# A fused attention and two-layer feed-forward kernel: 29 of 36 second-layer weight pieces converted inside the second layer, three a step, and used straight from SBUF

## The chip, the cores and the metric

One NeuronCore of one Trainium2 chip runs the whole program; the other cores are idle. The metric is the time of one execution on the device in microseconds (us), and the number compared is the median of several runs. Engines are called as in the profile: PE is TensorE (matmuls; PEld is its weight load), DVE is VectorE, ACT is ScalarE, POOL is GpSimd, SP is SyncE, which issues the DMAs. SBUF is the on-chip memory, PSUM the accumulators that PE writes, DRAM the memory off the core.

## The reference

Four batches of 512 tokens and 32 state rows pass through an attention block, then through two feed-forward layers. The first has 2048 hidden features and a softplus, the second 1536 hidden features, gated.

```python
def _moe_ref(x, w_in, w_out):                       # d_model 512, d_ff 2048
    h = x @ w_in
    g = np.maximum(h, 0.0) + np.log1p(np.exp(-np.abs(h)))
    return (g @ w_out).astype(np.float32)

def _moe2_ref(x, w_gate, w_val, w_out):             # d_model 512, d_ff 1536
    g = x @ w_gate
    silu = g * (1.0 / (1.0 + np.exp(-g)))
    val = x @ w_val
    return (silu * val @ w_out).astype(np.float32)

def reference(**kwargs):
    ...
    x = np.ascontiguousarray(attn_out.transpose(0, 2, 1, 3)).reshape(B * S, H * D)
    x = _moe_ref(x=x, **moe_kwargs)
    return _moe2_ref(x=x, **moe2_kwargs)
```

The weight matrices arrive as float64 and have to be turned into numbers that the engines can multiply; that conversion is what the change moves.

## The kernel before, in words

**Arithmetic.** PE multiplies in a reduced format (float32r). To keep float32 accuracy every operand is held as two parts, a high part and a low part (the remainder), and each product is three matmuls (`mm3`, L90): high by high, low weight by high, high weight by low. Making a pair costs one ACT copy for the high part and one subtraction for the low part (`low`, L93), on POOL for all weights.

**Weight pieces.** A raw piece is a 128x512 block of float64 words (512 KB) in SBUF, loaded by SP. Its conversion has named steps: `size` (ACT, L133 or L135), `head` and `tail` (DVE integer operations on the two 32-bit words), `high` (ACT, L164), `low` (POOL). There are two ways to convert. The first, used in the first layer, takes one head and two tails on DVE (L144, L155, L158). The second, called `slope`, takes one head and one tail (L139, L151). A gate piece (`gv`) of the second layer also needs `sums` (four 128x128 combinations of its quarters, L205; on DVE in the slope way, else on POOL) and `split_sums` (ACT, then POOL): the second layer multiplies two by two blocks with seven products in place of eight, and these are the combined weights. An output piece (`w2`) has no sums. For each of the 12 feature blocks f of the second layer there are two gate pieces, gv f_0 and gv f_1, and one output piece, w2 f: 36 in all.

**First layer.** 64 units (4 chunks of hidden features, 4 batches, 4 feature blocks each), each with a product into `ph` and one into `py`. Between chunks and batches DVE adds `yacc<-py` (L511) and makes `m` (L93), an operand of PE's next `ph`. The list EARLY puts 18 second-layer pieces at chosen units.

**Second layer.** Two passes of 12 steps (two batches a pass). Each step runs seven products of 6 matmuls on PE, in the order P1, P5, P2, P6, two output products (`po`), P7, state, two output products, P4, P3; steps 0 and 1 have a shorter order. P1, P6, P7 and P4 go into `px`, P5 and P3 into `pz`, P2 into `py`. ACT copies `px` after P1 (cA, L1025), after P6 (cB, L1054) and after P7 (cC, L1061); the next product into `px` has to wait for the copy. DVE adds `py` to cA (L1051), which ACT puts through SiLU (L1056), adds `pz` to cC (L1065) and, in the next step, finishes cA (L1069) and cB (L1077); POOL multiplies (L985). A step takes about 17 us. P5 of step n multiplies the operands T_0s and T_1s by split_gv n_0 and split_gv n_1.

The other 18 pieces are converted in steps 0 to 8, two a step. All 36 are stored to DRAM (`gv_d`, `w2_d`), and every step of both passes loads its operands back from there (`load_gw`, `load_w2`), into 8 `gw` and 4 `w2` slots. In steps 10, 12, 13, 14 and 16 a job named OutSums makes combined output weights for the second pass: two adds on DVE (`w2t`, L265), four on POOL (`w2u`, L276), then two high parts on ACT and two low parts on POOL (`w2o`). In steps 9 to 11 the operands of the second pass are combined as well (L527 and L531 on DVE, L529 and L533 on POOL).

**Order.** On DVE, ACT, POOL and SP the instructions run in the order in which the code is written (`manual_schedule`), through hooks: `at(n, kind, fn)` for units, `at2(n, kind, fn)` for steps, with conv0 to conv3 as the four points of a step. An instruction that waits holds all behind it on its engine.

Of the kernel before, what the change touches and what calls it, by code (L numbers as in the profile page):

```python
# [9 lines left out]
F32R = mybir.dt.float32r  # L10
# [6 lines left out]
P = 128  # L17
# [20 lines left out]
def attention_moe_moe2_kernel(  # L38
# [21 lines left out]
    NCK = F1 // CH  # L60
# [31 lines left out]
    def low(eng, o, whole, high):  # L92
        eng.tensor_tensor(out=o, in0=whole, in1=high.bitcast(F32), op=ALU.subtract)  # L93
# [22 lines left out]
    class Piece:  # L116
# [44 lines left out]

        def high(self):
            self.out = slot([P, 2, 512], F32R, self.tag, self.name)
            nc.scalar.activation(self.out[:, 0, :], self.t, AF.Copy)  # L164
# [17 lines left out]
    class GatePiece(Piece):  # L182
        def __init__(self, f, i, slope):
            cols = slice(f * P, (f + 1) * P)
            views = [w[(h + i) * P:(h + i + 1) * P, cols] for h in (0, 2) for w in (w_gate, w_val)]
            super().__init__(views, "made", f"gv{f}_{i}", "raw", slope)
            self.f, self.i = f, i
            if i == 0:
                gv_d[f] = dram.tile([P, 2, 2, 2, 512], F32, tag=f"gv{f}", name=f"gv{f}_d")

        def low(self):
            super().low()
            nc.sync.dma_start(out=gv_d[self.f][:, self.i, 0], in_=self.out.bitcast(F32))
# [13 lines left out]
        def split_sums(self):  # L207
            o = slot([P, 2, 512], F32R, "made", f"split_{self.name}")
            nc.scalar.activation(o[:, 0, :], self.s, AF.Copy)  # L209
            low(nc.gpsimd, o[:, 1, :], self.s, o[:, 0, :])  # L210
            nc.sync.dma_start(out=gv_d[self.f][:, self.i, 1], in_=o.bitcast(F32))

    class OutPiece(Piece):
        def __init__(self, f, slope):
            super().__init__([w_out2[f * P:(f + 1) * P, :]], "made", f"w2{f}", "raw", slope)
            self.f = f
            w2_d[f] = dram.tile([P, 2, 512], F32, tag=f"w2{f}", name=f"w2{f}_d")

# [12 lines left out]
    def second_piece(j, slope=False):  # L231
        f, part = divmod(j, 3)
        return OutPiece(f, slope) if part == 2 else GatePiece(f, part, slope)
# [504 lines left out]
    with tc.manual_schedule(engines={ENG.PE}):  # L738
# [63 lines left out]
        def at(n, kind, fn, *args):  # L802
            hooks.setdefault((n, kind), []).append((fn, args))
# [45 lines left out]
        EARLY = [(c * UC + n, 0) for c in range(NCK - 1) for n in ((2, 3, 6, 7, 10, 14) if c else (11, 14, 15))]  # L849
        EARLY += [((NCK - 1) * UC + n, 0 if n % 4 else 2) for n in (0, 1, 2)]  # L850
        for j, (n, late) in enumerate(EARLY):
            at_weights(n, late, made, (j,), second_piece)
            at(n + late + 1, "pool", lambda j=j: made[j,].sums())
            at(n + late + 2, "act", lambda j=j: made[j,].split_sums())
# [19 lines left out]
        for n in range(2):  # L874
            at(NU - 3 + n, "load", load_w2, n)
# [45 lines left out]
        for k, j in enumerate(range(len(EARLY), 3 * NF)):  # L921
            n, half = divmod(k, 2)

            def begin(j=j):
                made[j,] = second_piece(j, True)

            def step(name, j=j):
                return lambda: getattr(made[j,], name)()

            at2(n - 1, f"load{half}", begin)  # L930
            for late, names in enumerate((("head", "size"), ("tail",), ("high", "low"), ("sums",), ("split_sums",))):
                t = 4 * n + 2 * half + late + (late == 4)
                for name in names:
                    own = t // 4 >= 2 and t % 4 == 0 and name in ("size", "high", "low", "split_sums")
                    at2(t // 4, "copied" if own else f"conv{t % 4}", step(name))
# [196 lines left out]
```

## Time and profile before

| | value |
|---|---|
| median of 3 runs (lowest, highest) | 732.83 us (731.96, 732.92) |
| the profiled execution | 732.92 us, span 731.1 us |
| PE busy | 710.4 us, 97% of the span |
| DVE, ACT, POOL busy | 484.2, 331.0, 412.6 us (66%, 45%, 56%) |
| granted clock of PE, mean over the span | 0.993 |
| moved by DMA | 159.54 MB, mean 218 GB/s |
| loads of gate operands from DRAM, `gw<-gv_d` | 96 of 512 KB, 6.9 us from issue to landing |

The profiled execution is 0.09 us above the median, and 1.8 us of it lie outside the span. Busy time counts an instruction from its start to its end; the time in which an engine waits for another is idle.

### The profile page before, as it was taken

Reading aid. Unit: us, or ns where it says so; the run is one execution under the profiler, and the core shown is the slowest. Engines: PE = TensorE matmul, PEld = TensorE weight load, DVE = VectorE, ACT = ScalarE, POOL = GpSimd, SP = SyncE. Lnnn points to the kernel's source line nnn. Section 1 sums busy time; section 2 is a strip of 40 time slices with the busy share of each in tenths; the row PEclk is TensorE's granted clock in tenths of the full one; section 3 lists DMA queues with packets and bytes.
Section 4 is the critical chain, followed back from the end, with each engine's and each line's share of the span. In section 5 each row is a group of like instructions: output and inputs, shape, how many; then the busy total and the mean of one; then the engine's idle time right before and its main releaser. Section 6 shows DMA issues by size and latency. Waiting matters only on the chain.

```text
span 731.1 us, 10299 instructions
## 1 busy us (share of the span) xinstructions
PE 710.4 (97%) x3690; PEld 569.6 (78%) x3690; DVE 484.2 (66%) x689; ACT 331.0 (45%) x612; POOL 412.6 (56%) x349
## 2 busy tenths in 40 slices
PE   4899999999999999999999999999999999999997
PEld 1467877788777777788888888888888888888886
DVE  4884577888667866458476757665575665675564
ACT  3776365544445544434554344442443434333231
POOL 2477538877547765744265445455766567254352
PEclk9899999999999999999999999999999999999999
DMA  9930134655545535480389997879669997849503
GB/s 342 408 129 10 48 115 138 201 205 179 162 131 189 188 120 161 161 301 0 122 280 330 373 362 278 327 260 337 207 251 386 345 338 279 296 144 328 168 12 116
DMA packets 55395, 159.54 MB, mean 218 GB/s; under 512 B 6192, under 2 KB 18480, under 8 KB 55344
## 3 DMA queue, kind: packets, MB, share of 16 engines
q1 hardware_dynamic: 55344, 158.88, 61.4%
q8 instruction: 29, 0.48, 0.3%
q14 instruction: 22, 0.18, 0.1%
HBM read 117.70 MB, written 41.16 MB: 217 GB/s over the span
## 4 chain that ended last, share of the span: by engine, by line
PE 85%; DVE 8%; POOL 2%; issue 2%; ACT 2%; DMA 1%; SPq 0%; ACTq 0%; DVEq 0%; POOLq 0%
PE py L90 24%; PE px L90 18%; PE po L90 10%; PE ph L90 10%; PE pz L90 9%; PE poP L90 7%; PE pt L90 3%; PE pm L432 2%; PE ps L90 1%; PE ps L565 1%; DMA st<-in_st_dram 1%; DVE t_wo L155 1%; DVE t L351 1%; DVE m L93 1%; DVE m L354 1%
## 5 line engine op out<-in xcount | busy, mean ns | idle before, releaser
L90 PE MATMUL py<-h,wo 128*128 128x512 f32 x512 | 159.1, 391 | 0.6 <-POOL wo L93 0.6
L93 POOL TENSOR_TENSOR l<-C,h 128x512 fp32r<-128x512 f32 x64 | 91.7, 1439 | 78.7 <-ACT C L465 61.9
L90 PEld LDWEIGHTS py<-h,wo 128*128 128x128 f32 x512 | 95.9, 188 | 22.2 <-POOL wo L93 1.4
L90 PE MATMUL ph<-aT,m 128*128 128x512 f32 x384 | 99.9, 396 | 2.7 <-DVE m L93 2.7
L90 PE MATMUL py<-l,wo 128*128 128x512 f32 x256 | 99.9, 390 | 0.0
L90 PEld LDWEIGHTS ph<-aT,m 128*128 128x128 f32 x384 | 70.5, 188 | 28.0 <-issue 5.9
L462 ACT ACTIVATE h<-ph 128x512 fp32r<-128x512 f32 x64 | 38.2, 598 | 108.4 <-PE py L90 101.6
L90 PE MATMUL po<-h,w 128*128 128x512 f32 x224 | 69.7, 392 | 0.0
L90 PE MATMUL px<-T_0s,gw 128*128 128x512 f32 x216 | 60.8, 390 | 0.5 <-ACT cA L1025 0.5
L90 PE MATMUL px<-T_1s,gw 128*128 128x512 f32 x216 | 60.7, 390 | 0.0
L90 PEld LDWEIGHTS py<-l,wo 128*128 128x128 f32 x256 | 48.1, 188 | 10.2
L643 DVE TENSOR_TENSOR oacc<-po,oacc 128x512 f32<-128x512 f32 x48 | 32.4, 687 | 27.9 <-PE po L90 27.8
L90 PEld LDWEIGHTS po<-h,w 128*128 128x128 f32 x224 | 41.6, 188 | 8.4
L93 POOL TENSOR_TENSOR gv<-t_gv,gv 128x512 fp32r<-128x512 f32 x24 | 32.4, 1348 | 27.4 <-ACT gv L164 27.2
L643 DVE TENSOR_TENSOR oacc<-poP,oacc 128x512 f32<-128x512 f32 x62 | 40.7, 686 | 10.3 <-PE poP L90 10.3
L90 PEld LDWEIGHTS px<-T_0s,gw 128*128 128x128 f32 x216 | 40.4, 188 | 9.1 <-ACT cA L1025 1.0
L90 PEld LDWEIGHTS px<-T_1s,gw 128*128 128x128 f32 x216 | 40.6, 188 | 8.4
L90 PE MATMUL po<-l,w 128*128 128x512 f32 x112 | 43.7, 390 | 0.0
L93 POOL TENSOR_TENSOR split_gv<-sums_gv,split_gv 128x512 fp32r<-128x512 f32 x24 | 33.1, 1378 | 17.2 <-ACT split_gv L209 16.5
L93 POOL TENSOR_TENSOR l<-cA,h 128x512 fp32r<-128x512 f32 x14 | 19.7, 1407 | 40.0 <-ACT h L629 39.8
L985 POOL TENSOR_TENSOR cC<-cC,cB 128x512 f32<-128x512 f32 x24 | 31.8, 1326 | 18.4 <-ACT cB L984 18.4
L1051 DVE TENSOR_TENSOR cA<-py,cA 128x512 f32<-128x512 f32 x22 | 15.2, 689 | 40.2 <-PE py L90 34.1
(206 smaller groups left out, 1525.5 us busy)
## 6 DMA issues: line engine op xcount, KB each, us to landing
gw<-gv_d SPq DMA_DIRECT2D x96, 512.0 KB, 6.9
gv_d<-gv SPq DMA_DIRECT2D x24, 512.0 KB, 3.4
gv_d<-split_gv SPq DMA_DIRECT2D x24, 512.0 KB, 3.0
w<-w_d SPq DMA_DIRECT2D x24, 512.0 KB, 8.7
raw_win<-in_moe_w_in_dram SPq DMA_DIRECT2D x16, 512.0 KB, 6.9
raw_wo<-in_moe_w_out_dram SPq DMA_DIRECT2D x16, 512.0 KB, 4.3
raw_gv<-in_moe_w_gate_dram SPq DMA_DIRECT2D x48, 128.0 KB, 3.3
raw_gv<-in_moe_w_val_dram SPq DMA_DIRECT2D x48, 128.0 KB, 3.1
```

The source lines that it names most:

```text
L90: nc.tensor.matmul(o, a[s], b[t], start=first and i == 0, stop=last and i == 2, **k)
L93: eng.tensor_tensor(out=o, in0=whole, in1=high.bitcast(F32), op=ALU.subtract)
L155: nc.vector.scalar_tensor_tensor(out=ti, in0=self.top, scalar=-0x80000000, in1=ti, op0=ALU.bitwise_and, op1=ALU.bitwise_or,)
L351: nc.vector.transpose(self.t, self.sc)
L354: nc.vector.tensor_reduce(out=self.mine("m1", 16), in_=self.t3, op=ALU.max, axis=AX.X)
L432: nc.tensor.matmul(ps[k * NS:(k + 1) * NS, :], st[q, k, b, :], win[c, k].t[q, :], start=True, stop=True)
L462: nc.scalar.activation(self.h, self.ps, AF.Softplus)
L565: nc.tensor.matmul(gs[c][:, f], win[c, kt].t[:, f], sw[:, kt, :], start=kt == 0, stop=kt == KT - 1)
L643: nc.vector.tensor_tensor(out=v, in0=ps, in1=v, op=ALU.add)
L985: nc.gpsimd.tensor_tensor(out=c["C"], in0=c["C"], in1=c["B"], op=ALU.mult)
L1051: nc.vector.tensor_tensor(out=c["A"], in0=y, in1=c["A"], op=ALU.add)
```

## The change

Only 7 pieces stay in the first layer: gv0_0, gv0_1, gv1_0 and gv1_1 at units 38, 39, 42 and 46, then gv2_0, gv2_1 and w2 0 at units 48 to 50. The other 29 are converted in the second layer: piece gv f_0 begins two steps before step f at conv0, gv f_1 at conv1, w2 f at conv3, so that three are under way in a step, from step 0 (w2 1, w2 2, gv3_0, gv3_1) to step 11. Such a piece is written into a `gw` or `w2` slot itself (there are 10 and 5 now) and PE reads it there in the first pass. It is still stored to DRAM, and the second pass loads it. In the first pass only the operands of steps 0, 1 and 2 and w2 0 are loaded from DRAM.

```diff
-    SLOTS = {..., "w2": 4, "w2s": 4, "gw": 8}
+    SLOTS = {..., "w2": 5, "w2s": 4, "gw": 10}
...
+        def place(self):
+            return "gw" if self.slope else "made"
+
         def low(self):
             super().low()
+            if self.slope:
+                gw[self.f, self.i, 0] = self.out
             nc.sync.dma_start(out=gv_d[self.f][:, self.i, 0], in_=self.out.bitcast(F32))
...
         def split_sums(self):
-            o = slot([P, 2, 512], F32R, "made", f"split_{self.name}")
+            o = slot([P, 2, 512], F32R, self.place(), f"split_{self.name}")
             nc.scalar.activation(o[:, 0, :], self.s, AF.Copy)
             low(nc.gpsimd, o[:, 1, :], self.s, o[:, 0, :])
+            if self.slope:
+                gw[self.f, self.i, 1] = o
...
-        EARLY = [(c * UC + n, 0) for c in range(NCK - 1) for n in ((2, 3, 6, 7, 10, 14) if c else (11, 14, 15))]
+        EARLY = [((NCK - 2) * UC + n, 0) for n in (6, 7, 10, 14)]
         EARLY += [((NCK - 1) * UC + n, 0 if n % 4 else 2) for n in (0, 1, 2)]
...
+        for f in range(NF):
+            for part, t0 in enumerate((4 * f - 8, 4 * f - 7, 4 * f - 5 if f > 1 else 2)):
+                if (f, part) in made:
+                    continue
...
+                at2(t0 // 4 - 1, "load", begin)
+                for late, names in enumerate((("head", "size"), ("tail",), ("high", "low"), ("sums",), ("split_sums",))):
+                    t = t0 + late + (late == 4)
...
                 run2(n, "P3")
-                if n + 2 < NS2:
+                if n == 0 or NF <= n + 2 < NS2:
                     load_gw(n + 2)
-                if n % 2 and n + 1 < NS2:
+                if n % 2 and NF <= n + 1 < NS2:
                     load_w2(n + 1)
                     load_w2(n + 2)
```

Line numbers in the changed kernel are higher by up to 14: L205 is L213, L209 L217, L265 L279, L276 L290, L1025 L1038, L1051 L1064, L1069 L1082, L1077 L1090.

**First place: the end of the third batch of chunk 1, on DVE.** In the names, wo and win are first-layer weights. Before, the rows ahead of the operand `m` of the next product are:

```order
L155 SCALAR_TENSOR_TENSOR t_wo2_0_1747<-raw_wo2_0_1575,t_wo2_0_1747 128x512
L158 SCALAR_TENSOR_TENSOR t_wo2_0_1747<-raw_wo2_0_1575,t_wo2_0_1747 128x512
L155 SCALAR_TENSOR_TENSOR t_gv2_1_1826<-raw_gv2_1_1674,t_gv2_1_1826 128x512
L158 SCALAR_TENSOR_TENSOR t_gv2_1_1826<-raw_gv2_1_1674,t_gv2_1_1826 128x512
L511 TENSOR_TENSOR yacc2_0_1156<-py1_2_0_1751,yacc2_0_1156 128x512
...
L93 TENSOR_TENSOR m2_0_0_1867<-pm2_0_0_1843,m2_0_0_1867 128x512
```

With the change the same place on DVE reads:

```order
L155 SCALAR_TENSOR_TENSOR t_wo2_0_1613<-raw_wo2_0_1477,t_wo2_0_1613 128x512
L158 SCALAR_TENSOR_TENSOR t_wo2_0_1613<-raw_wo2_0_1477,t_wo2_0_1613 128x512
L525 TENSOR_TENSOR yacc2_0_1140<-py1_2_0_1617,yacc2_0_1140 128x512
L525 TENSOR_TENSOR yacc2_0_1140<-py1_2_1_1618,yacc2_0_1140 128x512
...
L93 TENSOR_TENSOR m2_0_0_1714<-pm2_0_0_1691,m2_0_0_1714 128x512
```

The two tails of gv2_1 are gone from between the tails of the first-layer piece and the adds.

**Second place: step 1 to step 2, on DVE and ACT.** Before, on DVE, around the row that finishes cA of step 1, and after it on ACT up to the copy that P6 of step 2 waits for:

```order
L151 SCALAR_TENSOR_TENSOR t_w26_3553<-t_w26_3553,raw_w26_3399 128x512
L139 TENSOR_SCALAR raw_gv7_0_3402<-raw_gv7_0_3402 128x512
L1069 TENSOR_TENSOR cA1_3514<-px1_3517,cA1_3514 128x512
```

```order
L164 ACTIVATE w26_3594<-t_w26_3553 128x512
L133 ACTIVATE t_gv7_0_3599<-raw_gv7_0_3402 128x512
L629 ACTIVATE h1_0_3608<-cA1_3514 128x512
L209 ACTIVATE split_gv6_1_3618<-sums_gv6_1_3584 128x512
L1025 ACTIVATE cA2_3647<-px2_3650 128x512
```

With the change, on DVE and then on ACT:

```order
L151 SCALAR_TENSOR_TENSOR t_gv3_0_3347<-t_gv3_0_3347,raw_gv3_0_3191 128x512
L139 TENSOR_SCALAR raw_gv3_1_3197<-raw_gv3_1_3197 128x512
L151 SCALAR_TENSOR_TENSOR t_gv3_1_3380<-t_gv3_1_3380,raw_gv3_1_3197 128x512
L1082 TENSOR_TENSOR cA1_3307<-px1_3310,cA1_3307 128x512
```

```order
L167 ACTIVATE gv3_0_3386<-t_gv3_0_3347 128x512
L643 ACTIVATE h1_0_3398<-cA1_3307 128x512
L167 ACTIVATE gv3_1_3413<-t_gv3_1_3380 128x512
L133 ACTIVATE t_w23_3418<-raw_w23_3202 128x512
L1038 ACTIVATE cA2_3435<-px2_3438 128x512
```

DVE now has two gate tails ahead of cA1 in place of one output tail and, before that, four sums; ACT has two operations between h1_0 and the copy cA2 in place of one.

**Third place: step 10, on DVE and POOL.** Before, on DVE from cA9 to cA10:

```order
L1069 TENSOR_TENSOR cA9_4798<-px9_4801,cA9_4798 128x512
L1077 TENSOR_TENSOR cB9_4799<-pz9_4811,cB9_4799 128x512
...
L265 TENSOR_TENSOR w2t0_0_4975<-w2r0_0_4794 128x512
L265 TENSOR_TENSOR w2t0_1_4977<-w2r0_1_4796 128x512
L1051 TENSOR_TENSOR cA10_4946<-py10_4966,cA10_4946 128x512
```

With the change, the same stretch of DVE (four sums of each gate piece, of which one stands here, lie at the two places marked):

```order
L1082 TENSOR_TENSOR cA9_4653<-px9_4656,cA9_4653 128x512
L213 TENSOR_TENSOR sums_gv11_0_4808<-t_gv11_0_4697 128x128
...
L139 TENSOR_SCALAR raw_w211_4487<-raw_w211_4487 128x512
L1090 TENSOR_TENSOR cB9_4654<-pz9_4666,cB9_4654 128x512
L213 TENSOR_TENSOR sums_gv11_1_4850<-t_gv11_1_4726 128x128
...
L151 SCALAR_TENSOR_TENSOR t_w211_4818<-t_w211_4818,raw_w211_4487 128x512
L541 TENSOR_TENSOR T3_1_1_4856<-yacc3_1_1323,yacc3_0_1320 128x512
L279 TENSOR_TENSOR w2t0_0_4858<-w2r0_0_4649 128x512
L279 TENSOR_TENSOR w2t0_1_4860<-w2r0_1_4651 128x512
L1064 TENSOR_TENSOR cA10_4823<-py10_4843,cA10_4823 128x512
```

And POOL with the change, in the same step (before, the rows of split_gv11 and w211 lie in step 9, and POOL has T4 (L533), cC9, L529, the four w2u, l9_1 and the two w2o here):

```order
L1000 TENSOR_TENSOR cC9_4655<-cC9_4655,cB9_4654 128x512
L93 TENSOR_TENSOR split_gv11_0_4887<-sums_gv11_0_4808,split_gv11_0_4887 128x512
L93 TENSOR_TENSOR w211_4891<-t_w211_4818,w211_4891 128x512
L543 TENSOR_TENSOR yacc3_0_1320<-yacc3_0_1320,yacc2_0_1140 128x512
L290 TENSOR_TENSOR w2u0_0_4896<-w2t0_0_4858,w2t0_1_4860 128x256
...
L93 TENSOR_TENSOR l9_1_4910<-cC9_4655,h9_1_4909 128x512
L93 TENSOR_TENSOR split_gv11_1_4933<-sums_gv11_1_4850,split_gv11_1_4933 128x512
L93 TENSOR_TENSOR w2o0_0_4939<-w2u0_0_4896,w2o0_0_4939 128x512
```

The conversion of the last gate pieces now stands in the same step as the first OutSums job, and split_gv11_1, an operand of P5 in step 11, is POOL's last row before the two w2o. On ACT the high part of split_gv11_0 stands right behind the SiLU of cA10.

## Rows read from the trace of the kernel before

**Rows 1.** Windows of 20 us: busy us (instructions) by engine, clock, DMA share, GB/s.

```profile
60.00:80.00 20.00, 20.00 (x100) 15.65 (x99) 9.43 (x17) 12.29 (x22) 13.13 (x12) 1.00 0.09 27
...
180.00:200.00 20.00, 19.30 (x113) 15.49 (x112) 14.23 (x20) 10.27 (x19) 10.94 (x12) 1.00 0.44 136
...
260.00:280.00 20.00, 19.24 (x103) 14.98 (x101) 12.79 (x18) 8.65 (x16) 12.07 (x12) 1.00 0.53 162
...
360.00:380.00 20.00, 19.47 (x94) 16.12 (x93) 14.05 (x26) 11.01 (x21) 12.09 (x9) 1.00 0.83 293
...
700.00:720.00 20.00, 20.00 (x90) 16.56 (x89) 12.01 (x18) 6.50 (x12) 9.56 (x8) 1.00 0.03 11
```

**Rows 2.** Waits of PE: us in total, times, longest.

```profile
PE ph L90 <- DVE m L93: 2.7, 3, 1.3
```

**Rows 3.** Timeline, 178 to 186 us, DVE and PE: start, duration, operation [idle before].

```profile
178.91 1.77 DVE L155 SCALAR_TENSOR_TENSOR t_gv<-raw_gv,t_gv 128x512 int32<-128x512 int32 x1
...
183.72 1.28 DVE L93 TENSOR_TENSOR m<-pm,m 128x512 fp32r<-128x512 f32 x2
184.55 1.63 PE L90 MATMUL ph<-aT,m 128*128 128x512 f32 x6 [0.70 <-DVE m L93]
```

**Rows 4.** Timeline, 368 to 374 us (step 1 to step 2), four engines.

```profile
367.25 0.28 DVE L205 TENSOR_TENSOR sums_gv<-t_gv 128x128 f32<-128x128 f32 x1
...
368.65 1.34 POOL L93 TENSOR_TENSOR l<-cC,h 128x512 fp32r<-128x512 f32 x1
368.77 1.37 DVE L205 TENSOR_TENSOR sums_gv<-t_gv 128x128 f32<-128x128 f32 x1
...
370.27 0.68 DVE L151 SCALAR_TENSOR_TENSOR t_w<-t_w,raw_w 128x512 int32<-128x512 int32 x1
370.87 0.42 DVE L139 TENSOR_SCALAR raw_gv<-raw_gv 128x512 int32<-128x512 int32 x1
371.20 0.68 DVE L1069 TENSOR_TENSOR cA<-px,cA 128x512 f32<-128x512 f32 x1
373.11 0.58 ACT L1025 ACTIVATE cA<-px 128x512 f32<-128x512 f32 x1
373.74 0.97 PE L90 MATMUL px<-T_0s,gw 128*128 128x512 f32 x3 [0.53 <-ACT cA L1025]
```

**Rows 5.** Lines by form, 370 to 520 us, DVE: busy us, mean ns | idle before.

```profile
L205 DVE TENSOR_TENSOR sums_gv<-t_gv 128x128 f32<-128x128 f32 x21 | 8.8, 420 | 0.0
L151 DVE SCALAR_TENSOR_TENSOR t_gv<-t_gv,raw_gv 128x512 int32<-128x512 int32 x10 | 8.8, 876 | 0.4 <-ACT t_gv L133 0.3
L151 DVE SCALAR_TENSOR_TENSOR t_w<-t_w,raw_w 128x512 int32<-128x512 int32 x6 | 8.5, 1420 | 0.0
L139 DVE TENSOR_SCALAR raw_gv<-raw_gv 128x512 int32<-128x512 int32 x10 | 8.4, 835 | 2.8 <-DMA raw_gv<-in_moe_w_val_dram 2.8
```

**Rows 6.** Lines by form, 370 to 520 us, POOL.

```profile
L93 POOL TENSOR_TENSOR split_gv<-sums_gv,split_gv 128x512 fp32r<-128x512 f32 x11 | 16.3, 1479 | 1.1 <-ACT split_gv L209 1.1
```

**Rows 7.** Timeline, 506 to 527 us (steps 10 and 11), and a later w2t pair.

```profile
506.40 0.69 DVE L1069 TENSOR_TENSOR cA<-px,cA 128x512 f32<-128x512 f32 x1 [0.67 <-PE px L90]
509.65 3.48 DVE L265 TENSOR_TENSOR w2t<-w2r 128x512 f32<-128x512 f32 x2
513.05 0.68 DVE L1051 TENSOR_TENSOR cA<-py,cA 128x512 f32<-128x512 f32 x1
513.77 0.63 ACT L1056 ACTIVATE cA<-cA 128x512 f32<-128x512 f32 x1
514.24 0.74 POOL L276 TENSOR_TENSOR w2u<-w2t,w2t 128x256 f32<-128x256 f32 x1
525.58 0.84 PE L90 MATMUL pz<-T_0s,gw 128*128 128x512 f32 x3
526.26 0.84 PE L90 MATMUL pz<-T_1s,gw 128*128 128x512 f32 x3
602.90 1.28 DVE L265 TENSOR_TENSOR w2t<-w2r 128x512 f32<-128x512 f32 x2
```

More of the change, by code (lines that the diff above doesn't have):

```diff
@@ L160, in tail @@
             )
+        def place(self):
+            return self.tag
         def high(self):
-            self.out = slot([P, 2, 512], F32R, self.tag, self.name)
+            self.out = slot([P, 2, 512], F32R, self.place(), self.name)
             nc.scalar.activation(self.out[:, 0, :], self.t, AF.Copy)
@@ L182, in attention_moe_moe2_kernel, with __init__ @@
     class GatePiece(Piece):
-        def __init__(self, f, i, slope):
+        def __init__(self, f, i, late):
             cols = slice(f * P, (f + 1) * P)
             views = [w[(h + i) * P:(h + i + 1) * P, cols] for h in (0, 2) for w in (w_gate, w_val)]
-            super().__init__(views, "made", f"gv{f}_{i}", "raw", slope)
+            super().__init__(views, "made", f"gv{f}_{i}", "raw", late)
             self.f, self.i = f, i
@@ L207, in split_sums, with __init__, place @@
         def split_sums(self):
-            o = slot([P, 2, 512], F32R, "made", f"split_{self.name}")
+            o = slot([P, 2, 512], F32R, self.place(), f"split_{self.name}")
             nc.scalar.activation(o[:, 0, :], self.s, AF.Copy)
             low(nc.gpsimd, o[:, 1, :], self.s, o[:, 0, :])
+            if self.slope:
+                gw[self.f, self.i, 1] = o
             nc.sync.dma_start(out=gv_d[self.f][:, self.i, 1], in_=o.bitcast(F32))
     class OutPiece(Piece):
-        def __init__(self, f, slope):
-            super().__init__([w_out2[f * P:(f + 1) * P, :]], "made", f"w2{f}", "raw", slope)
+        def __init__(self, f, late):
+            super().__init__([w_out2[f * P:(f + 1) * P, :]], "made", f"w2{f}", "raw", late)
             self.f = f
             w2_d[f] = dram.tile([P, 2, 512], F32, tag=f"w2{f}", name=f"w2{f}_d")
+        def place(self):
+            return "w2" if self.slope else "made"
         def low(self):
             super().low()
+            if self.slope:
+                w2[self.f] = self.out
             nc.sync.dma_start(out=w2_d[self.f], in_=self.out.bitcast(F32))
@@ L229, in attention_moe_moe2_kernel, with second_piece @@
     made = {}
-    def second_piece(j, slope=False):
-        f, part = divmod(j, 3)
-        return OutPiece(f, slope) if part == 2 else GatePiece(f, part, slope)
+    def second_piece(f, part, late=False):
+        return OutPiece(f, late) if part == 2 else GatePiece(f, part, late)
     gw = {}
@@ L847, in attention_moe_moe2_kernel @@
             at(i, kind, fn, 0)
-        EARLY = [(c * UC + n, 0) for c in range(NCK - 1) for n in ((2, 3, 6, 7, 10, 14) if c else (11, 14, 15))]
+        EARLY = [((NCK - 2) * UC + n, 0) for n in (6, 7, 10, 14)]
         EARLY += [((NCK - 1) * UC + n, 0 if n % 4 else 2) for n in (0, 1, 2)]
[L851 to L854, printed above, removed]
+        for key, (n, late) in zip(((0, 0), (0, 1), (1, 0), (1, 1), (2, 0), (2, 1), (0, 2)), EARLY):
+            at_weights(n, late, made, key, second_piece)
+            at(n + late + 1, "pool", lambda key=key: made[key].sums())
+            at(n + late + 2, "act", lambda key=key: made[key].split_sums())
         n0 = (NCK - 1) * UC + FT
@@ L873, in attention_moe_moe2_kernel @@
             at(NU - 5 + n, "load", load_gw, n)
-        for n in range(2):
-            at(NU - 3 + n, "load", load_w2, n)
+        at(NU - 3, "load", load_w2, 0)
         with tc.manual_schedule(engines={ENG.DVE, ENG.SP, ENG.Activation, ENG.Pool}):
@@ L919, in run2, with begin @@
                 fn(*args)
[L921 to L935, printed above, removed]
+        for f in range(NF):
+            for part, t0 in enumerate((4 * f - 8, 4 * f - 7, 4 * f - 5 if f > 1 else 2)):
+                if (f, part) in made:
+                    continue
+                def begin(f=f, part=part):
+                    made[f, part] = second_piece(f, part, True)
+                at2(t0 // 4 - 1, "load", begin)
+                for late, names in enumerate((("head", "size"), ("tail",), ("high", "low"), ("sums",), ("split_sums",))):
+                    t = t0 + late + (late == 4)
+                    for name in names:
+                        own = t // 4 >= 2 and t % 4 == 0 and name in ("size", "high", "low", "split_sums")
+                        at2(
+                            t // 4, "copied" if own else f"conv{t % 4}",
+                            lambda f=f, part=part, name=name: getattr(made[f, part], name)(),
+                        )
         for p in range(1, NPR):
```

11 lines of the change are left out of this document (5 added, 6 removed).

## The prediction

> **What bounds the kernel now.** I read the windows of 20 us first. PE is busy for all 20.00 us of every window from 60 to 720 us, at a clock of 1.00, except in three, where 0.70, 0.76 and 0.53 us are missing [rows 1]. So almost nothing can be won beside PE, and the change leaves PE's own instructions as they are: the same matmuls in the same order, with another buffer as the weight. What it can give is at most those three gaps, 1.99 us; what it can cost is any wait that it makes PE take.
>
> Then I asked what ended each gap. PE waited three times for DVE's `m`, 2.7 us in all [rows 2]. The longest, 1.3 us, lies in the start, before any second-layer piece; the other two are the first two gaps above. At 184.55 us PE had waited 0.70 us for an `m` that DVE began at 183.72; before it DVE had done the two tails of a second-layer piece, the first in 1.77 us, and the four yacc adds [rows 3]. The third gap is ACT's copy cA at 373.11 us in step 2, for which P6 waited 0.53 us [rows 4].
>
> Last I looked at how DVE and POOL treat each other, since the change puts more of both into each step of the second layer's first pass. A sum of gate weights takes 0.28 us at 367.25, and 1.37 us at 368.77, when POOL's subtraction runs from 368.65 for 1.34 us [rows 4]. The same shows in the mean of a tail, 0.88 us for a gate and 1.42 for an output piece [rows 5], where a free one takes 0.68 [rows 4]. So DVE work between SBUF operands stands still during part of a POOL operation.
>
> **The change, part by part.**
>
> *First layer, gain 0.7.* No second-layer piece is left in chunk 1, so the two tails of gv2_1 go from between DVE's earlier work and `m`. The first alone took 1.77 us [rows 3], more than the 0.70 us of the wait; I count the whole 0.70 as gained. In chunk 2, unit 42 keeps a gate piece, so the gap of 0.76 us stays. The rest of what leaves the first layer is off PE's path and worth nothing: every window there is full. Units 38 and 46 get a gate piece in place of an output piece, so POOL has four sums and one subtraction of about 1.5 us [rows 6] more at each, in a window where it is busy for 12.07 of 20 [rows 1]: nothing there.
>
> *DMA, 0.* Some 45 reloads of 512 KB go from the first pass. None of the three gaps ended at a DMA, though the window of the third moved 293 GB/s [rows 1], so this is worth nothing either way. The raw pieces are loaded one step, 17 us, ahead of their head, against the 6.9 us of a reload in the table above.
>
> *Step 1 to step 2, cost 0.3.* On DVE, from 367.25 on, a gate tail, a head and another gate tail now stand ahead of cA1. Free they take 0.68 + 0.42 + 0.68 = 1.8 us [rows 4], at the mean 0.88 + 0.84 + 0.88 = 2.6 [rows 5], blocked 1.77 + 0.84 + 1.77 = 4.4 [rows 3, 5]. So cA1 starts at 369.1, 369.9 or 371.7; before it was 371.20 [rows 4]. Behind cA1 (0.68 us) ACT has h1_0, the high part of gv3_1, the size of w23 and then the copy cA2: three operations of about 0.63 us, so the copy starts 2.6 us after cA1. P6 stands ready 0.53 us before the old copy would let it, so a copy at 373.11 − 0.53 = 372.6 costs nothing and the wait is cA1's start less 370.0: from 0 to 1.7, against 0.53 now. Two of the three prices are near, the tails' neighbours on POOL are two (w22 and l0_1), and I take the middle, cA1 at 370.8 and a wait of 0.8: a cost of 0.3, bounds −0.5 and +1.2.
>
> *Steps 3 to 9, cost 0.5.* A step gets two gate pieces and one output piece in place of 4/3 and 2/3. A gate piece costs DVE 0.84 + 0.88 + four sums of 0.28 to 0.42, some 3.1 us, an output piece 0.84 + 1.42 = 2.3 [rows 5]; the step gains 2/3 of one and 1/3 of the other, 2.8 us. POOL gains 2/3 × 2 × 1.48 + 1/3 × 1.4 = 2.4 us. The fullest window before has DVE at 14.05 and POOL at 12.09 of 20 [rows 1], that is 11.9 and 10.3 in a step of 17 us; with the additions 14.7 and 12.7. Both still fit, so no rate is lost; what can happen is that one operation comes late within a step. In nine steps before that happened once, for 0.53 us. I take once more 0.5; bounds 0 and 0.5 a step, 3.5.
>
> *Steps 10 and 11, cost 2.0.* This is the place that decides. Before, the gate pieces of step 11 were done in step 9, and DVE had one T and the w2t pair between cA9 and cA10's add. Now it has there eight sums, a head, a tail, the T, the w2t pair and the cB9 add. Free: 8 × 0.28 + 0.42 + 0.68 + 0.68 + 1.28 + 0.68 = 6.0 us [rows 4, 7]. From the end of cA9, 507.1, that reaches 513.1, the very time at which the add stood before [rows 7]. But POOL has four operations here (l9_0, gv11_1, T4, cC9) of 1.34 to 1.48 us, 5.6 together [rows 4, 6]. The w2t pair took 3.48 us at 509.65 under the same POOL load, and 1.28 when free [rows 7], so 2.2 of 3.48 us, 0.63, went to blocking. 0.63 × 5.6 = 3.5: cA10's add starts at 516.6 and ends at 517.3. The SiLU takes 0.63 to 517.9, the high part of split_gv11_0 behind it as long, to 518.5. Then POOL, in order: split_gv11_0, w211, an yacc add, four w2u of 0.74, l9_1, split_gv11_1. Five of 1.34 to 1.48 and 2.96 make 9.7 to 10.4 us: split_gv11_1 is there at 528.2 to 528.9. PE's P5 of step 11 begins at 525.58, its second half, which takes split_gv11_1, at 526.26, and the low part is used in the second of its three matmuls, at 526.5 [rows 7]. The wait is 1.7 to 2.4; I take 2.0. Bounds: with no blocking the chain is 3.5 us earlier and the wait 0; with DVE blocked for all 5.6 us it is 2.1 longer, and one more if DVE enters step 10 late: 5.
>
> The Trainium skill ("SBUF — State Buffer", section "SBUF: two separate sides") calls the port pair of GpSimd and the Vector engine an exclusive lock: who starts first holds it for the whole instruction, and a DVE operation with two SBUF inputs is "fully" blocked. By that rule the blocked share would be 1 rather than 0.63 and the wait in step 11 about 4.1; the sum row at 368.77 agrees in kind, the w2t pair lies between.
>
> *After that.* The loads of step 12 come behind the stores of w2o on SP, which now wait for split_gv11_1 and two w2o, until about 531. They take 6.9 us, to 538 or later; step 12 starts at about 542 plus the wait. Covered, by some 3 us.
>
> **The sum.** The profiled execution is 732.92 us (0.09 above the median): −0.7 + 0.3 + 0.5 + 2.0 = +2.1, so 735.0 us. A measurement of this kernel can tell about 0.2%, 1.5 us, from no change: slower begins at 734.3, faster at 731.4.
>
> **Rivals.**
>
> *Covered after all: no difference.* DVE gets through step 10 between POOL's operations, cA10's add is at 514.5 or earlier, and split_gv11_1 is there in time. For it: the free sum ends exactly at the old time. Against it: the pair's 3.48 us. Time 732.92 − 0.7 + 0.3 + 0.5 = 733.0. It decides where the add starts before 514.9.
>
> *Faster.* POOL has fewer second-layer operations in the first layer and DVE is blocked less by it, so that the wait for `m` in chunk 2 goes too, and the copy in step 2 is in time. Then all three gaps close, and if steps 3 to 11 add none: 732.92 − 1.99 = 730.9. For it: such a tail took 1.77 us where a free one takes 0.68 [rows 3, 4]. Against it: a gate piece still stands at unit 42, and POOL has no less to do near it. It decides where `m` comes 0.76 us earlier there.
>
> *Saturated.* DVE's and POOL's SBUF work hardly overlap, so that they fill the step: DVE's share of such work free, three heads, three tails and eight sums, 3 × 0.42 + 3 × 0.68 + 8 × 0.28 = 5.5 us, and POOL's 12.7 make 18.2 against 17, and a step loses up to 1.2 us, 8 steps 9.6. Half of it on the sum: 735.0 + 4.8 = 739.8. Against it: POOL's 12.7 already holds its own blocked time.
>
> *The reload of step 12 is late.* If its cover of 3 us goes, PE waits in step 12 as well; 2 us on the sum, 737.0.
>
> **How the numbers follow.** Forecast 0.45 (0.07 of it within 0.2% of no change), covered 0.27 (0.02 of it slower), faster 0.13, saturated 0.09, late reload 0.06. So slower is 0.38 + 0.02 + 0.09 + 0.06 = 0.55, same 0.07 + 0.25 = 0.32, faster 0.13. The likeliest case by itself spans 733.5 to 738; the range that leaves out 2 in 10 reaches from the faster case to near the saturated one: 731.2 to 739.5.
>
> **What would show it.** In the changed profile: no wait of PE for `m` at about 184 us; one for ACT's cA at about 373 us, of 0 to 1.7; DVE busy some 2.8 us more in each step of the first pass; cA10's add 2 to 5 us later against the start of its step; and a wait of PE's `pz` (P5) for POOL's split_gv in step 11, of 0 to 5 us. Wrong it would be if PE waits in each of steps 3 to 9, or for a DMA, or nowhere.

## The result

The changed kernel takes 737.6 us, the median of 4 runs (736.61 to 739.45), against 732.88 us for the kernel before (4 runs, 731.96 to 733.89): a ratio of 1.0067, 95% interval 1.0043 to 1.0091. It is slower, by 4.7 us where 2.1 was forecast, and inside the range of 731.2 to 739.5. The profiled execution took 737.51 us, with a span of 735.7, 4.6 more than before.

The page of the changed kernel has nearly the same work as before on every engine (busy us, share of the span, instructions), so nearly all of the 4.6 us are waits (POOL has less to do, since the sums that left the first layer went to DVE):

```profile
PE 710.5 (97%) x3690; PEld 569.3 (77%) x3690; DVE 486.7 (66%) x702; ACT 328.3 (45%) x611; POOL 401.4 (55%) x325
```

The windows of the changed kernel, in the columns of [rows 1], show where PE is not full between 60 and 720 us: three windows again, but not the same three.

```profile
180.00:200.00 20.00, 20.00 (x116) 16.22 (x116) 8.04 (x14) 8.66 (x16) 6.56 (x5) 1.00 0.18 53
...
260.00:280.00 20.00, 16.84 (x89) 12.72 (x88) 15.05 (x20) 8.92 (x17) 12.23 (x12) 1.00 0.45 135
...
360.00:380.00 20.00, 19.21 (x91) 15.83 (x90) 14.88 (x23) 11.24 (x21) 12.27 (x9) 1.00 0.58 188
...
400.00:420.00 20.00, 20.00 (x96) 16.81 (x95) 19.51 (x28) 11.58 (x22) 15.18 (x12) 1.00 0.67 223
...
520.00:540.00 20.00, 18.29 (x91) 15.22 (x90) 13.82 (x15) 11.60 (x23) 18.86 (x16) 1.00 0.53 172
```

The gap at 184 us is closed. At 260 us 3.16 us are missing where it was 0.76 [rows 1], at 360 us 0.79 against 0.53, at 520 us 1.71 where PE was full. The gaps grew from 1.99 to 5.66 us, by 3.7. PE's matmuls end 4.5 us later in all, and 1.0 us of that stands already at 62 us, in the start. What is left over, 0.2 us to the good, comes in steps of some 0.2 us that the windows do not show: between 147 and 244 us PE gains 0.9 us in such steps beside the gap at 184, and later it loses 0.7. The waits of PE in the changed kernel that answer to [rows 2] name what ended them:

```profile
PE ph L90 <- DVE yacc L525: 2.3, 1, 2.3
PE pz L90 <- POOL split_gv L93: 1.7, 1, 1.7
...
PE py L90 <- DVE m L93: 0.8, 1, 0.8
PE px L90 <- ACT cA L1038: 0.8, 1, 0.8
```

**Step 11** went as forecast. The timeline of the changed kernel, steps 10 and 11, to be held against [rows 7] with 2.36 us added (P5 begins at 527.94, where it was 525.58):

```profile
509.63 0.68 DVE L1082 TENSOR_TENSOR cA<-px,cA 128x512 f32<-128x512 f32 x1
511.16 1.52 DVE L139 TENSOR_SCALAR raw_w<-raw_w 128x512 int32<-128x512 int32 x1
512.60 0.68 DVE L1090 TENSOR_TENSOR cB<-pz,cB 128x512 f32<-128x512 f32 x1
515.20 1.38 DVE L213 TENSOR_TENSOR sums_gv<-t_gv 128x128 f32<-128x128 f32 x1
519.11 0.68 DVE L1064 TENSOR_TENSOR cA<-py,cA 128x512 f32<-128x512 f32 x1
...
515.09 1.34 POOL L1000 TENSOR_TENSOR cC<-cC,cB 128x512 f32<-128x512 f32 x1
521.06 1.30 POOL L93 TENSOR_TENSOR split_gv<-sums_gv,split_gv 128x512 fp32r<-128x512 f32 x1 [4.63 <-ACT split_gv L217]
529.40 1.27 POOL L93 TENSOR_TENSOR split_gv<-sums_gv,split_gv 128x512 fp32r<-128x512 f32 x1
...
527.94 0.84 PE L90 MATMUL pz<-T_0s,split_gv 128*128 128x512 f32 x3
530.72 0.73 PE L90 MATMUL pz<-T_1s,split_gv 128*128 128x512 f32 x2 [1.72 <-POOL split_gv L93]
```

The add to cA10 starts 8.8 us ahead of P5 (forecast 9.0), the second split follows the first by 8.3 us of POOL work and ends at 530.67, and PE waits 1.72 us in the second half of P5 (forecast 1.7 to 2.4). **Step 2**, likewise in the changed kernel (P6 of step 2 stood at 373.74 before):

```profile
371.60 1.59 DVE L151 SCALAR_TENSOR_TENSOR t_gv<-t_gv,raw_gv 128x512 int32<-128x512 int32 x1
373.12 0.68 DVE L1082 TENSOR_TENSOR cA<-px,cA 128x512 f32<-128x512 f32 x1
...
375.50 0.57 ACT L1038 ACTIVATE cA<-px 128x512 f32<-128x512 f32 x1
...
376.12 0.96 PE L90 MATMUL px<-T_0s,gw 128*128 128x512 f32 x3 [0.79 <-ACT cA L1038]
```

The copy starts 2.4 us after cA1 begins (forecast 2.6), and the wait is 0.79, as forecast. Counted from the moment at which PE is ready for P6, cA1 begins 0.2 us earlier than before, not later. The cost comes from ACT, whose copy follows cA1 by 2.4 us where it was 1.9 [rows 4]: two operations stand between h1_0 and the copy in place of one.

**The loss that was not forecast** is at 261 us, at the end of the third batch of chunk 2. The timeline of the changed kernel there:

```profile
253.25 0.46 POOL L213 TENSOR_TENSOR sums_gv<-t_gv,sums_gv 128x128 f32<-128x128 f32 x1
...
253.75 0.63 ACT L217 ACTIVATE split_gv<-sums_gv 128x512 fp32r<-128x512 f32 x1 [4.70 <-POOL sums_gv L213]
254.28 0.65 ACT L135 ACTIVATE t_gv<-raw_gv 128x512 f32<-128x512 f32 x1
...
255.04 1.00 DVE L144 TENSOR_SCALAR t_gv<-t_gv 128x512 int32<-128x512 int32 x1 [3.00 <-ACT t_gv L135]
261.13 1.63 DVE L158 SCALAR_TENSOR_TENSOR t_gv<-raw_gv,t_gv 128x512 int32<-128x512 int32 x1
262.69 2.47 DVE L525 TENSOR_TENSOR yacc<-py,yacc 128x512 f32<-128x512 f32 x4
...
263.42 1.66 PE L90 MATMUL ph<-aT,m 128*128 128x512 f32 x6 [2.34 <-DVE yacc L525]
265.90 0.69 PE L90 MATMUL py<-h,wo 128*128 128x512 f32 x2 [0.82 <-DVE m L93]
```

In the kernel before the same place reads as follows (PE begins `ps`, its work ahead of this `ph`, at 257.89 us there and at 257.35 here):

```profile
251.14 0.63 ACT L209 ACTIVATE split_gv<-sums_gv 128x512 fp32r<-128x512 f32 x1 [1.56 <-POOL sums_gv L205]
252.44 0.98 DVE L144 TENSOR_SCALAR t_gv<-t_gv 128x512 int32<-128x512 int32 x1 [2.48 <-ACT t_gv L135]
258.55 0.69 DVE L158 SCALAR_TENSOR_TENSOR t_gv<-raw_gv,t_gv 128x512 int32<-128x512 int32 x1
```

Read the changed kernel's rows from above. POOL ends the four sums of the piece at unit 39 at 253.7; ACT waits 4.7 us for them, to make the high part of that piece's split; behind that ACT has the size of the piece at unit 42; DVE's head waits 3.0 us for the size; behind the head stand four tails and the yacc adds, and PE waits for these. Each engine runs in its order, so one late sum on POOL is passed on through ACT and DVE to PE. The chain was there before too, but shorter: counted from PE's `ps`, the head now comes 3.1 us later, and the last tail, held by POOL's work, takes 0.9 us more. DVE is 4.1 us later with the yacc adds; the gap grows by 2.4 us of it, since PE now does its `ph` of 1.66 us between two waits.

### The profile page after: what moved, and what is told of

Its sections match the earlier page's. It is cut to its first block, busy times and chain, and to the rows that moved or that the text cites. A ratio compares the mean times of both kernels' runs of the same rounds, so it can differ in the third digit from the quotient of the medians.

```text
span 735.7 us, 10190 instructions
## 1 busy us (share of the span) xinstructions
PE 710.5 (97%) x3690; PEld 569.3 (77%) x3690; DVE 486.7 (66%) x702; ACT 328.3 (45%) x611; POOL 401.4 (55%) x325
## 4 chain that ended last, share of the span: by engine, by line
PE 89%; DVE 4%; POOL 3%; issue 1%; DMA 1%; ACT 1%; SPq 0%; ACTq 0%; DVEq 0%; POOLq 0%
PE py L90 26%; PE px L90 17%; PE ph L90 11%; PE po L90 10%; PE pz L90 8%; PE poP L90 6%; PE pt L90 3%; PE pm L446 2%; PE ps L90 1%; PE ps L579 1%; DMA st<-in_st_dram 1%; DVE mx L345 1%; POOL l L93 1%; POOL sums_gv L213 1%; POOL split_gv L93 1%
## 5 line engine op out<-in xcount | busy, mean ns | idle before, releaser
L93 POOL TENSOR_TENSOR l<-C,h 128x512 fp32r<-128x512 f32 x64 | 89.4, 1400 | 130.4 <-ACT C L479 114.4
L525 DVE TENSOR_TENSOR yacc<-py,yacc 128x512 f32<-128x512 f32 x48 | 32.0, 688 | 33.3 <-PE py L90 33.3
L90 PE MATMUL px<-T_0s,gw 128*128 128x512 f32 x135 | 38.1, 390 | 0.8 <-ACT cA L1038 0.8
L479 ACT ACTIVATE C<-ph 128x512 f32<-128x512 f32 x64 | 38.0, 594 | 0.0
L90 PE MATMUL px<-T_1s,gw 128*128 128x512 f32 x135 | 38.0, 389 | 0.0
L1064 DVE TENSOR_TENSOR cA<-py,cA 128x512 f32<-128x512 f32 x22 | 15.1, 684 | 31.2 <-PE py L90 23.5
L93 POOL TENSOR_TENSOR gv<-t_gv,gv 128x512 fp32r<-128x512 f32 x24 | 35.4, 1476 | 0.0
```

Of the source, the lines that this page charges most:

```text
L90: nc.tensor.matmul(o, a[s], b[t], start=first and i == 0, stop=last and i == 2, **k)
L479: nc.scalar.activation(self.g, self.ps, AF.Softplus)
L525: nc.vector.tensor_tensor(out=v, in0=yps[dt], in1=v, op=ALU.add)
L1064: nc.vector.tensor_tensor(out=c["A"], in0=y, in1=c["A"], op=ALU.add)
```

## The experiments

All were timed beside the kernel before on the same chip; that kernel's median in these three sets was 733.24, 733.38 and 733.56 us.

**What causes the wait at 261 us.** Two edits of the changed kernel. The first puts the output piece first among the early ones:

```diff
-        for key, (n, late) in zip(((0, 0), (0, 1), (1, 0), (1, 1), (2, 0), (2, 1), (0, 2)), EARLY):
+        for key, (n, late) in zip(((0, 2), (0, 0), (0, 1), (1, 0), (1, 1), (2, 0), (2, 1)), EARLY):
```

> The seven early pieces keep their units, but the output piece w2 0 goes first, to unit 38, and the six gate pieces follow at units 39 to 50; everything else as in the changed kernel. Theory: the 2.3 and 0.8 us that PE waits at 261 to 266 us come from the gate piece at unit 38 (a subtraction, four sums and a split more on POOL, 2.4 us late at unit 39's sums). Then an output piece there brings the waits back to about 0.8 us together and the time to 735.2 us. Rival: they come from the gate piece at unit 42 and DVE's tails alone, which stay; then no change, 737.6 us. The wait in step 11 stays at 1.7 in both.

It took 733.92 us (12 runs), a ratio of 1.0007, interval 0.9997 to 1.0018. One wait of 1.1 us is left there, and 1.7 in step 11. The theory gave 0.8 us of wait and 735.2 us, the rival 737.6, and ACT waits 0.9 us for the sums in place of 4.7: the gate piece at unit 38 does make them late. What is left is told by two rows of this run:

```profile
249.81 1.06 DVE L144 TENSOR_SCALAR t_gv<-t_gv 128x512 int32<-128x512 int32 x1 [2.00 <-ACT t_gv L135]
250.55 3.17 POOL L93 TENSOR_TENSOR l<-C,h 128x512 fp32r<-128x512 f32 x2
```

The head still waits for the size, and the four tails behind it run beside POOL's row of subtractions: they take 1.77, 1.67, 1.78 and 1.65 us. The second edit moves one ACT operation of 0.65 us:

```diff
             for m, kind, step in (
-                (n - 1, "act1", "size"), (n, "dve0", "head"), (n + late, "dve1", "tail"),
+                (n - 2 if store is made and n % UC == 10 else n - 1, "act1", "size"), (n, "dve0", "head"), ...
```

> The changed kernel with one ACT operation put sooner: the size of the gate piece at unit 42 is issued a unit earlier, ahead of the high part of split_gv0_1 rather than behind it. Theory: ACT runs in order, that high part waits for POOL's four sums, the size behind it is late, so DVE's head and all tails and yacc adds behind it are late, and PE waits. Then the waits at 261 to 266 us fall from 3.2 us to under 1, 735 us or a little less. Rival: DVE is late because POOL blocks its tails (1.6 to 1.8 us each, four of them), wherever the size stands; then the waits stay above 2 us and the time at about 737.

It took 733.41 us (11 runs), 1.0004, interval 0.9994 to 1.0014: some 4 us less than the change, with nothing else moved (3.2 us is the wait itself; what it can cost beside that stands in the last section). The timeline of this run at the same place:

```profile
247.67 0.66 ACT L135 ACTIVATE t_gv<-raw_gv 128x512 f32<-128x512 f32 x1
...
254.44 0.63 ACT L217 ACTIVATE split_gv<-sums_gv 128x512 fp32r<-128x512 f32 x1 [5.14 <-POOL sums_gv L213]
...
251.68 0.68 DVE L144 TENSOR_SCALAR t_gv<-t_gv 128x512 int32<-128x512 int32 x1
254.99 0.69 DVE L158 SCALAR_TENSOR_TENSOR t_gv<-raw_gv,t_gv 128x512 int32<-128x512 int32 x1
255.60 2.47 DVE L525 TENSOR_TENSOR yacc<-py,yacc 128x512 f32<-128x512 f32 x4
...
260.55 1.62 PE L90 MATMUL ph<-aT,m 128*128 128x512 f32 x6
```

ACT still waits 5.1 us for POOL's sums, which are even later, but the size is past it; DVE ends its tails 7 us sooner, since they begin some 3 us sooner and then meet less of POOL's work (0.69 against 1.63 us for the last), and PE does not wait at all. So the chain through ACT carries the wait, as the theory had it. DVE's blocked tails, the rival, are a part of it, and an early head alone does not free them: in the run before, the head began 9.9 us ahead of the time at which PE was ready for its next `ph`, here 8.9 us, and there the tails were blocked in full and PE waited 1.1 us. Here they are through before POOL, itself late, begins that row.

**What holds step 11.** The split of gv11_1 a point sooner:

```diff
-                    t = t0 + late + (late == 4)
+                    t = t0 + late + (late == 4 and (f, part) != (NF - 1, 1))
```

> The changed kernel with the split of gate piece gv11_1 issued one point of step 10 earlier, so that POOL does it right behind split_gv11_0 and ahead of w211, the yacc add, the four w2u and l9_1. Theory: PE's 1.7 us wait in step 11 is the length of that POOL row (some 7 us ahead of the split). Then split_gv11_1 is there at about 524 us by the clock of the changed kernel's profile, 5 us before its use, the wait is 0, the time 735.9 us. Rival: DVE's late cA10 add holds the whole step, and another operand takes its place (ACT's copy cC10 ahead of P4, or the loads of step 12 behind the w2o stores): a wait of 1 to 2 us elsewhere in steps 10 to 12, 737 us.

It took 737.47 us (6 runs), 1.0062, interval 1.0046 to 1.0078: nothing gained. Both sides were half right. The wait of 1.7 us in P5 of step 11 is gone, so POOL's row ahead of the split did make it; but two others took its place, before P6 and before P3, the last product of the same step:

```profile
530.57 0.96 PE L90 MATMUL px<-T_0s,split_gv 128*128 128x512 f32 x3 [0.37 <-ACT cA L1038]
...
544.66 0.96 PE L90 MATMUL pz<-B_0s,split_gv 128*128 128x512 f32 x3 [1.43 <-DVE cC L1078]
```

Both still multiply by a split of gv11, so step 12 has none. Behind POOL's w2u stand ACT's two w2o, behind these the copy cA11 and the operands of the second pass. To take that away too, the first OutSums job goes to step 11, together with the edit of the size:

```diff
-        for q, n in enumerate((10, 12, 13, 14, 16)):
+        for q, n in enumerate((11, 12, 13, 14, 16)):
```

> The changed kernel with the size at unit 42 put sooner, as in the run that removed the waits at 261 us, and with the first OutSums job moved from step 10 to step 11 (two w2t on DVE, four w2u and two w2o on POOL, two high parts on ACT). Theory: with the split alone moved forward the wait came back in steps 11 and 12 because ACT's two w2o stood behind POOL's w2u and held the copy cA11 and the operands of the second pass; with the whole job out of step 10 neither is late. Then no wait in step 11, under 0.5 us in step 12, and 733.4 - 1.9 = 731.5 us. Rival: DVE and POOL have simply too much to do in steps 10 to 12, so the job in step 11 delays cC11 and P3 by as much; then 733 to 734 us.

It took 734.29 us (12 runs), 1.0013, interval 0.9999 to 1.0026, not 731.5. In step 11 only 0.2 us are left, before P3, and step 12 has no wait, so the theory held there and the rival's cC11 did not come; but in step 13 PE waits 1.7 us for a copy of ACT, and later 0.2 for a load. The timeline of this run shows ACT at the second w2o of the next job:

```profile
558.80 0.63 ACT L295 ACTIVATE w2o<-w2u 128x512 fp32r<-128x512 f32 x1 [7.84 <-DVE w2t L279]
...
559.86 0.58 ACT L1038 ACTIVATE cA<-px 128x512 f32<-128x512 f32 x1
```

It waited 7.8 us for a w2t, an operation of the job after its own, which had itself waited 2.6 us for a DMA. Nothing in the arithmetic asks for that; the likely reason is that the automatic allocation put that w2o on the bytes of a tile which the w2t reads. That is argued from the rows and was not tried by itself.

**What holds step 2.** The run before, and ACT's size of w23 behind the copy cA2:

```diff
+                        if (f, part, name) == (3, 2, "size"):
+                            at2(2, "P1", lambda f=f, part=part: made[f, part].size())
+                            continue
                         at2(
                             t // 4, "copied" if own else f"conv{t % 4}",
```

> As the run before it, and ACT's size of w23 issued behind the copy cA2 of step 2 rather than ahead of it. Theory: the wait of 0.8 us before P6 of step 2 is cA1's lateness plus the ACT operations between h1_0 and the copy, so it falls by the 0.65 us of that size to about 0.3 and the time by 0.6 against the run before. Rival: the copy waits for DVE's cA1 and its followers whatever stands between; then the wait stays at 0.8.

It took 731.42 us (11 runs), 0.9975, interval 0.9963 to 0.9987: 0.25% faster than the kernel before, little but clear of the noise. The wait for the copy in step 2 is down to 0.2 us, as the theory had it. Of the other 2 us against the run before, 1.7 come from step 13, where the w2o no longer waits, though ACT has the same operations there in the same order. That fits other addresses, which are not shown. The waits of PE after the start in this run are the whole of what is left:

```profile
PE px L90 <- ACT cA L1041: 0.2, 1, 0.2
PE pz L90 <- DVE cC L1081: 0.2, 1, 0.2
PE px L90 <- ACT cB L1070: 0.2, 1, 0.2
```

**Half of the change undone.** EARLY as before, with 18 pieces; only features 6 to 11 used straight from SBUF:

```diff
-        EARLY = [((NCK - 2) * UC + n, 0) for n in (6, 7, 10, 14)]
+        EARLY = [(c * UC + n, 0) for c in range(NCK - 1) for n in ((2, 3, 6, 7, 10, 14) if c else (11, 14, 15))]
...
-                if n == 0 or NF <= n + 2 < NS2:
+                if n + 2 < 6 or NF <= n + 2 < NS2:
```

> Half of the change undone: the 18 early pieces of the kernel before stay in the first layer and are loaded from DRAM, the other 18 (features 6 to 11) are converted three a step in steps 4 to 11 and used straight from SBUF. Theory: what the change costs comes from where the pieces stand, in three places. Then the first layer is as before (waits of 0.7 and 0.8 us at its two places), the wait in step 2 goes, the one in step 11 stays at 1.7: 732.9 - 0.5 + 1.7 = 734.1 us. Rival: three pieces a step wear DVE and POOL down over the whole first pass, or the use from SBUF itself costs (slots held longer): then PE waits in several of steps 4 to 9 as well, 736 us or more.

It took 738.24 us (6 runs), 1.0072, interval 1.0052 to 1.0091, 4 us more than the theory gave. In the second layer the theory holds: no wait in step 2, none in steps 4 to 10, 1.7 us in step 11 (and 0.2 at a load in the second pass). In the first layer it does not: the waits are larger than in the kernel before, although the order on DVE, ACT and POOL there is the same. Windows of this run (a third gap, of 0.6 us, lies at 146 us, where PE was full before):

```profile
180.00:200.00 20.00, 19.19 (x112) 15.41 (x111) 14.41 (x20) 9.04 (x17) 11.81 (x11) 1.00 0.47 143
260.00:280.00 20.00, 17.97 (x104) 14.30 (x104) 14.23 (x18) 8.61 (x16) 13.24 (x12) 1.00 0.43 128
```

Whether the same chain carries these is told by the edit of the size on this kernel and on the kernel before, at units 26 and 42 (the diff is that of the second run above).

> The half-undone kernel (18 early pieces, the other 18 used straight from SBUF) with the same edit at units 26 and 42. It had waits of 0.5, 1.0 and 2.2 us in the first layer though its instructions stand there in the order of the kernel before; only the addresses of the tiles differ. Theory: the same chain carries them, set off by an earlier ACT copy; then all but a few tenths go, 738.2 - 3.2 = 735.0 us, with the 1.7 us of step 11 left. Rival: the other addresses make DVE and POOL late by themselves; then more than half of the 3.7 us stays, 736.5 or more.

> The kernel before with the same one edit: the size of the gate pieces at units 26 and 42 issued a unit sooner on ACT. Theory: its two gaps of 0.7 and 0.8 us at 184 and 262 us come from the same chain (POOL's sums, ACT's high part of the split, the size behind it, DVE's head and all behind it), so both go and the time falls by 1.5 us, 0.2%, without any of the change. Rival: in the kernel before they come from the tails alone; then both gaps stay and the time is the same.

The first took 733.63 us (11 runs), 1.0003, interval 0.9995 to 1.0012: 4.6 us less, with PE at 20.00 us in both windows. The second took 731.59 us (8 runs), 0.9973, interval 0.9962 to 0.9984: its windows are full too.

```profile
180.00:200.00 20.00, 20.00 (x116) 16.23 (x116) 12.29 (x17) 10.27 (x19) 12.15 (x12) 1.00 0.50 151
260.00:280.00 20.00, 20.00 (x118) 14.97 (x116) 10.09 (x14) 9.68 (x19) 11.98 (x12) 1.00 0.58 180
```

So the gaps behind units 26 and 42 hang on that one ACT operation, in the change, in the half-undone kernel and in the kernel before. The gap at 146 us of the half-undone kernel does not: it is still 0.6 us after the edit, and what makes it was not followed. The kernel before gets from this edit alone (0.9973) what the change gets with three (0.9975).

**The start.** Both kernels were profiled a second time.

> The kernel before, unchanged, profiled a second time. Of the 4.5 us by which the changed kernel's matmuls end later, 1.0 us stands already at 50 us, in the start, where neither program has a second-layer piece. If that is the start's own scatter, this profile's first 50 us differ from the first profile's by some tenths to one us; if the kernel before always starts alike, they agree within 0.2 us and the 1.0 us belongs to the change.

> The changed kernel, unchanged, profiled a second time. Its first profile was 1.0 us later than the kernel before at 50 us already; the kernel before differed by 0.2 between its two profiles. If the 1.0 us belongs to the changed program, it stands here again, within 0.3 us; if it is scatter of the start, this profile is some tenths to one us off the first, while the waits at 261, 375 and 529 us repeat within 0.2 us.

The same group of matmuls stands at 77.97 and 77.82 us in the two profiles of the kernel before, and at 78.99 and 78.66 in those of the changed kernel. The expectation for the changed kernel set 0.3 us as the limit and the difference is 0.33: that pair does not settle whether the 0.7 to 1.0 us belong to the change. The other profiles do. The kernel before with the size moved, whose start is that of the kernel before, has the group at 78.77; the five edits of the changed kernel that keep its start have it at 77.27 to 78.75, on both sides of the kernel before. So the start scatters by more than the difference, and the 1.0 us of the first profile is not shown to be the change's. The waits at 375 and 529 us repeat within 0.1 us; the one at 261 repeats as well, and cost more, as told below.

## Why the prediction was right, and where it was not

*What bounds the kernel*: right. PE is full outside the gaps in all kernels, and the change in time is PE's gaps and the start, but for those steps of 0.2 us.

*First layer, gain 0.7*: right at its place, the gap at 184 us is closed. The reason was half of it: the prediction took the length of the two tails, and in the kernel before with the size moved the same gap closes with both tails still there. Wrong in the next sentence: "unit 42 keeps a gate piece, so the gap of 0.76 us stays", and of the gate piece at unit 38 "nothing there", because POOL was busy for 12.07 of 20 us in that window. This is the step that failed. The gap grew to 3.16 us, so 2.4 us were left out of the sum. The window was not the right one either: 12.07 belongs to 260 to 280 us, and POOL converts the piece of unit 38 at 242 to 248, in a window in which it was already busy for 15.00 us before, and is for 17.34 with the change:

```profile
240.00:260.00 20.00, 20.00 (x109) 15.75 (x108) 16.35 (x20) 10.91 (x20) 15.00 (x13) 1.00 0.55 185
240.00:260.00 20.00, 20.00 (x112) 16.07 (x111) 13.89 (x12) 10.90 (x21) 17.34 (x17) 1.00 0.52 183
```

But even the right share says nothing of what waits for the one operation that comes late: POOL's sums of unit 39 end after a gate piece more, and ACT, DVE and PE take the delay on in turn. ACT's order shows it (the size stands behind the split's high part). The prediction read ACT's order for steps 2 and 10, and not for this place. The rival "faster" had the sign wrong here: it expected DVE to be blocked less at unit 42. And what else left the first layer, put at nothing because every window is full, gave PE 0.7 to 0.9 us in steps of some 0.2 (three pairs of profiles, each with and without the change).

*DMA, 0*: right. The loads of gate operands from DRAM fell from 96 to 60, and no wait that went was one for them.

*Step 1 to step 2, cost 0.3*: measured 0.79 against 0.53, 0.26. Both halves were right, cA1 no later than before and one ACT operation more behind it.

*Steps 3 to 9, cost 0.5*: 0; no wait of PE there in any run. DVE's busy time grew more than the 2.8 us a step: in the window from 400 us it went from 14.53 (more than the 14.05 that the prediction took for the fullest) to 19.51 of 20, and from 380 to 520 us by 4.9 us a step of 17. POOL's grew by 2.5, as forecast. Nearly full and often held by POOL, DVE still was on time; the rival "saturated" fell by that.

*Steps 10 and 11, cost 2.0*: 1.72. The path was right, from DVE's row to cA10's add, through SiLU, high part and POOL's chain, to P5. That the add came within 0.2 us of the forecast is partly luck, for two errors cancel. DVE entered the step 0.9 us late (cA9 begins 18.3 us ahead of P5 where it was 19.2 before), which stood only in the upper bound. And its free row takes 5.1 us rather than 6.0, since in these rows an operation begins before the one ahead of it ends. The blocked time is 3.7 us (forecast 3.5): the head and three sums take 1.52, 0.78, 1.26 and 1.38 us, free ones 0.42 and 0.28.

The Trainium skill's rule ("SBUF — State Buffer", section "SBUF: two separate sides") of an exclusive lock gave 4.1 us. Operation by operation the rows agree with it: a sum of 0.28 us takes 1.38 at 515.20, until POOL's multiplication of 1.34 us at 515.09 is over. As a sum it was too much: POOL's four operations make 5.4 us and DVE lost 3.7 of them. In the rest it did cB9's add, which reads PSUM and took its free 0.68 at 512.60, and one held operation each time behind a POOL operation. The w2t pair, from which the share of 0.63 was taken, met no POOL work and took its free 1.28 us.

*The reload of step 12*: covered, as forecast; no wait for a DMA there.

The sum of the forecast's terms was 2.1; with 2.4 for chunk 2 and the measured sizes of the others, −0.70 + 2.40 + 0.26 + 0 + 1.72 = 3.7, which is what the windows show; the 1.0 us of the start comes on top, less the 0.2 in small steps. So the direction rests on the place that was forecast, step 11, but the largest term was put at nothing. That the time still lies inside the range is owed to its width, which was drawn from other terms.

## What to carry to other kernels

Where engines run in order, follow a piece of side work to the end of its chain: who waits for it, and what stands behind that waiting instruction on its engine, three engines on if need be. A producer can be late for one consumer although its engine has idle time: POOL was busy for 17.34 of 20 us there. And one moved operation of 0.65 us gave the kernel before 0.27%, where the whole change cost it 0.67%: take the wait's own cause away before moving work in bulk.

## What the runs showed of the hardware that was not expected

**A wait that costs twice.** In the second profile of the changed kernel PE waited as long at 263 us as in the first, but the granted clock fell behind it. Windows of that run, in the columns of [rows 1]:

```profile
260.00:264.00 4.00, 1.63 (x11) 1.30 (x10) 3.97 (x5) 2.04 (x4) 3.95 (x4) 1.00 0.01 2
264.00:268.00 4.00, 3.24 (x10) 2.26 (x9) 3.15 (x6) 0.27 (x1) 2.78 (x5) 0.57 0.51 166
268.00:272.00 4.00, 4.00 (x24) 2.03 (x22) 0.00 (x0) 1.08 (x2) 0.00 (x0) 0.58 0.29 96
272.00:276.00 4.00, 4.00 (x25) 3.19 (x18) 1.54 (x2) 2.15 (x4) 2.05 (x2) 1.00 0.00 0
```

PE waited 2.37 us, worked for 1.7 us and waited 0.76 us more. The granted clock fell between these two waits: from 265 to 271 us it was 0.50, the lower of the two levels, 1.2 GHz, and from 272 us 1.00 again, 2.4 GHz. That execution took 739.92 us with a span of 738.2, against 735.7 in the first profile, where the clock there stayed at 1.00. It is the same program, so a wait of this length was paid at two prices. The scatter of the changed kernel, 736.6 to 739.9 us, may come from this in part; only these two of its executions were profiled.

**The layout moves the time.** The half-undone kernel and the kernel before run the first layer in the same order, and lost 2.8 and 1.5 us in the same two windows, and 0.6 and nothing at 146 us. The addresses of the tiles differ between them, and with them which buffer an operation waits for; that this is the cause was not shown by itself.
